# Keys and queries of half batches 4 and 5: direct loads and TensorE transposes in place of casts and transposing loads

## The chip, the cores and the metric

The kernel runs on one core of a Trainium2 chip. A core has a matrix engine (TensorE, PE in the profile; PEld is its weight load), a vector engine (DVE), a scalar engine (ACT), GpSimd (POOL) and a sync engine (SP) that mostly issues DMA transfers. Each engine works through its own list of instructions in order; semaphores order the lists among each other. The metric is the device time of one execution in microseconds. The median of three runs of the kernel before is 398.96 us.

## The reference

Attention with a window of 32 positions to each side, and with 8 global positions that see everything and are seen by everything; then an MLP with the activation h cos(h).

```python
scores = (q @ k.T) / sqrt(D)                 # B, H, S, D = 8, 8, 576, 64
mask = (abs(i - j) <= 32) | is_global[i] | is_global[j]
attn = softmax(where(mask, scores, -1e9))
x = (attn @ v).transpose(0, 2, 1, 3).reshape(B * S, H * D)     # 4608 x 512
h = x @ w_in                                 # w_in 512 x 2048
out = (h * cos(h)) @ w_out                   # w_out 2048 x 512
```

All inputs and the output are float32 in DRAM; the kernel computes in float16 with float32 sums.

## The kernel before

A *pair* is two heads of one batch (32 pairs, `pr`), a *half* is four heads of one batch, so two pairs (16 halves, `s` or `n`). Half n holds pairs 2n and 2n + 1. Halves 4 and 5, which the change is about, hold pairs 8 to 11.

**Attention of one pair.** The queries are cut into 11 blocks of 56. For every block there is a tile of 128 keys (the 8 global ones and 120 around the block) in `kw`, and a tile of queries in `qb`. `scores` multiplies them four blocks at a time into a PSUM tile `st` (L440), ACT takes the exponential `e` (L442), and DVE multiplies it with a mask to `pm` (L443). `values` multiplies `pm` with the values `vw` into `pv` (L452), and DVE normalises to `xn` (L463). `turn_x` transposes `xn` on PE (L475), and DVE copies it into `xT` (L478), the transposed input of the MLP.

**MLP.** `mlp_in`, written "1" in the order, makes one 128 x 512 block of h (L491, four matmuls into `ph`), its cosine on ACT (L494) and the product `g` on DVE (L495). `mlp_out`, written "2", does four matmuls of the second layer into `po` (L505); each fourth one ends with a copy of `po` to `o` (L510 on ACT or L512 on DVE) and a store (L514).

**How kw and qb are filled.** Their 8 global columns come from POOL's copies (L394, L398, L399). The rest is made by `local_k` and `local_q` in one of two ways. For pairs below `2 * HY`, with HY = 4 the pairs 0 to 7, `load_qk` (L260, issued by POOL) brings a half's keys and queries into `kn` and `qn` with positions on partitions, 72 partitions of four heads of 8 rows, converted to float16 on the way. `turned` then transposes them on PE, 16 small transposes for k and 16 for q (L407) into a PSUM tile `t`; ACT copies k into `kw` (L414) and one head of q into `qb`, DVE the other head (L427). For the other pairs `cast_half` (L249 for v, L253 for k and q, issued by POOL) converts a half into float16 scratch in DRAM, `turn_half` (L265 and L266, issued by SP) loads k and q of it with a transposing DMA into `kT` and `qT`, and DVE copies from there (L417, L430).

**Values.** `load_v` and `load_vg` (L308 to L316, issued by SP) fill `vw` of a pair, four buffers in turn, from the scratch that the cast of v wrote, and from the gathered global rows.

**Order of the work.** The schedule is written by hand: the order of calls is the order of instructions on each engine. A first part (FRONT, L674) does pairs 0 to 3 and loads the weights. Then the loop at L684, called the steps here, runs s = 2 to 15; step s does the attention of pairs 2s and 2s + 1 between pieces of the MLP, in the order of the string ORDER (THIRD for s = 2). In it `sa0 sa1 sa2` and `sz0 sz1 sz2` are the scores of the two pairs, `pa` and `pz` their values, `xa` and `xz` their `turn_x`, `n` is a sum of squares on ACT (L524), `G` the casts, and `kc qc kd qd` prepare `kw` and `qb` for the two pairs of the next step. A "1" or "2" with nothing ready does nothing.

`G` is `casts(s)`: POOL waits for the `xn` of the step's second pair (L662), then issues the casts of half s + 2 (with s = 4 also of half 7, and the gather of the second half of the global rows). At the end of step s come `turn_half(s + 2)` and then the values of pairs 2s + 4 and 2s + 5, all on SP, whose list is in order: what stands behind a transposing load waits until the cast that it reads has landed.

PSUM tiles with the tag "s", three buffers in turn, hold `st`, the result of `turn_x` and, in the steps, also `t`. `po` has one buffer in the steps and `ph` has two.

Of the kernel before, what the change touches and what calls it, by code (L numbers as in the profile page):

```python
# [24 lines left out]
W = 120  # L25
BP = 6
KL = 32
HY = 4
RW = 8
KPAD = 4  # L30
KP = KPAD + S // RW + 10
# [23 lines left out]
def dview(ap, offset, *dims):  # L55

    return bass.AP(ap.tensor, ap.offset + offset, [list(d) for d in dims])
# [134 lines left out]
def kernel(  # L192
# [51 lines left out]
    def cast_half(s, which):  # L244

        base = s * 4 * S * D
        for x in which:
            if x == "v":
                nc.gpsimd.dma_start(v16[s * 4 * S : (s + 1) * 4 * S].rearrange("(n r) d -> n (r d)", r=16),  # L249
                                    dview(v, base, (16 * D, 4 * S // 16), (1, 16 * D)))  # L250
            else:
                src, dst = {"k": (k, k16), "q": (q, q16)}[x]
                nc.gpsimd.dma_start(dst[s].rearrange("t (h d) -> t h d", h=4),  # L253
                                    dview(src, base, (D, S), (S * D, 4), (1, D)))

    def load_qk(s):

        base = s * 4 * S * D
        for src, dst in ((k, kn[s % 2][KPAD : KPAD + S // RW]), (q, qn[s % 2][0 : S // RW])):
            nc.gpsimd.dma_start(dst.rearrange("x h r d -> x h (r d)"),  # L260
                                dview(src, base, (RW * D, S // RW), (S * D, 4), (1, RW * D)))

    def turn_half(s):

        nc.sync.dma_start(kT[s % 2][:, :, KL : KL + S], k16[s], transpose=True)  # L265
        nc.sync.dma_start(qT[s % 2][:, :, 0:S], q16[s], transpose=True)  # L266
# [19 lines left out]
    def gather(src, dst, half):  # L286
        rows = src.rearrange("b h s d -> (b h s) d")
        for h in range(2):
            nc.gpsimd.indirect_dma_start(
                out=dst[:, half, h], out_offset=None, in_=rows,  # L290
                in_offset=bass.IndirectOffsetOnAxis(ap=gidx_rows[:, 0:1], axis=0),
                element_offset=(half * 32 + h) * S * D)
# [80 lines left out]
    def build_globals(half):  # L373
        for src, dst in ((kg32, kgT), (qg32, qgT)):
            g16 = work.tile([P, P], FP16, tag="g16")
            nc.scalar.copy(g16, src[:, half].rearrange("x h d -> x (h d)"))
            t = ps.tile([P, 16 * G], FP16, tag="s", bufs=3)
            nc.tensor.transpose(t, g16, ident16)
            nc.scalar.copy(dst[:, 16 * half : 16 * half + 16], t.rearrange("x (n g) -> x n g", g=G))
        nc.scalar.copy(vg16[:, half], vg32[:, half])  # L380
# [20 lines left out]
    def turned(src, pr, n):  # L401

        t = ps.tile([P, RW, n], FP16, tag="h" if front[0] else "s", bufs=2 if front[0] else 3)
        h0 = 2 * (pr % 2)
        for r in range(RW):
            for h in range(2):
                nc.tensor.transpose(t[h * D : (h + 1) * D, r], src[:n, h0 + h, r], ident16[:n, :n])  # L407
        return t

    def local_k(pr):  # L410
        to = kw[pr % NK][:, :, G:]
        if pr < 2 * HY:
            t = turned(kn[pr // 2 % 2], pr, KP)
# [5 lines left out]
    def local_q(pr):  # L419
        if pr < 2 * HY:  # L420
            t = turned(qn[pr // 2 % 2], pr, QP)
        for h in range(2):
            hp = slice(h * D, (h + 1) * D)
            to = qb[pr % NK][hp, :, h, G:]
            if pr < 2 * HY:
                copy = nc.scalar.copy if h == 0 or pr < 2 else nc.vector.tensor_copy
                copy(view(to, (2 * C, NB), (RW, QB // RW), (1, RW)),  # L427
                     view(t[hp], (QB // RW, NB), (1, QB // RW), (QP, RW)))
            else:
                nc.vector.tensor_copy(to, view(qT[pr // 2 % 2][hp, pr % 2], (QB, NB), (1, QB)))  # L430
# [89 lines left out]
    def x_squares(s):  # L520

        sq = work.tile([P, 2 * BP * P], FP16, tag="sq", bufs=1)
        xn = xn_of.pop(s)
        nc.scalar.activation(sq, view(xn, (1, 2 * BP * P)), AF.Square,  # L524
                             accum_out=x_sq[:, s : s + 1])
# [47 lines left out]
    def one(n=1):  # L573
        for _ in range(n):

            if ins_q and ins_q[0][0] < ready[0] and ins_q[0][0] < outs_q[0][0] + 2:
                t, f = ins_q.pop(0)
                mlp_in(t, f)
                ready[1] = t * NF + f + 1

    def two(n=1):
        for _ in range(n):
            t, u = outs_q[0] if outs_q else (NTT, 0)

            need = min(t * NF + 4 * (u % 4) + 12, NTT * NF) if tail[0] else min(t * NF + 4 * (u % 4) + 7, (t + 1) * NF)
            if outs_q and need <= ready[1] and (tail[0] or NTT * NF - len(outs_q) < outs_by[0]):
                mlp_out(*outs_q.pop(0))
# [7 lines left out]
    with tc.manual_schedule():  # L595
# [48 lines left out]
        def load_values(pr):  # L644
            load_v(pr)
            load_vg(pr)
# [9 lines left out]
        def globals_kq(pr):  # L656
            globals_k(pr)
            globals_q(pr)

        def casts(s):  # L660

            nc.gpsimd.tensor_copy(gate, xn_of[s][0:1, 1, 0, 0:1])  # L662
            for n in range(4, 2 * B):
                if s == (n - 2 if n < 7 else n - 3):
                    cast_half(n, "vkq")
            if s == 4:
                for src, dst in ((k, kg32), (q, qg32), (v, vg32)):
                    gather(src, dst, 1)
# [15 lines left out]
        for s in range(2, B * NP // 2):  # L684
            if s == 2:
                nc.gpsimd.dma_start(w_out16, moe_w_out.rearrange("(c p) n -> p c n", p=P))
            outs_by[0] = 4 * (s - 2) if s < 5 else 8 * (s - 3)
            for pr in (2 * s + 2, 2 * s + 3):
                if 8 <= pr < B * NP:
                    globals_kq(pr)  # L690
            for step in (THIRD if s == 2 else ORDER).split():
                if step == "1":
                    one()
                elif step == "2":
                    two()
                elif step == "n":
                    x_squares(s - 1)
                elif step == "G":
                    casts(s)
                else:  # L700
                    f, pr = (STEPS | LOCAL)[step[0]], 2 * s + "azcd".index(step[1])
                    if pr < B * NP:
                        f(pr, *[int(x) for x in step[2:]])
            if s % 2 == 1:
                ready[0] = s // 2 + 1 + (s // 2 == B - 1)
            if s < B * NP // 2 - 2:
                turn_half(s + 2)
                load_values(2 * s + 4)
                load_values(2 * s + 5)
            if s == 5:  # L710
                build_globals(1)
# [49 lines left out]
```

## Time and profile before

The profiled execution has a span of 395.4 us from the first to the last instruction.

| | |
|---|---|
| median of the runs (lowest, highest) | 398.96 us (396.92, 400.0) |
| span of the profiled execution | 395.4 us |
| busy PE, DVE, ACT, POOL | 328.3, 260.6, 238.8, 114.8 us |
| matmuls of the MLP, L491 and L505 | 142.8 and 140.4 us, 576 each |
| transposes of k and q on PE, L407 | 5.7 and 5.3 us, 128 each |
| ACT copies from them, L414 and L427 | 8 x 1257 ns, 10 x 666 ns |
| DVE copies from them, L427 | 6 x 803 ns |
| DVE copies from kT and qT, L417 and L430 | 24 x 556 ns, 48 x 460 ns |
| POOL issuing casts of k and q, L253 | 12 x 1765 ns, 12 x 2304 ns |
| POOL issuing direct loads of k and q, L260 | 4 x 821 ns, 4 x 785 ns |
| DMA queue q1 (issued by SP) | 124,509 packets, 27.89 MB |
| DMA queue q0 (issued by POOL) | 63,952 packets, 18.75 MB |

How to read such a profile: a line of the engine groups names the line of the code, the engine, the operation and the tiles as output<-input; a timeline line begins with the start and the duration in us, and ends in brackets with the time that the engine stood idle before it and what it waited for. Steps 2 to 5 run from 55.47, 74.98, 99.68 and 118.22 us; step 6 begins at 140.05, and from step 8 on a step takes 16.9 us. The loop ends at about 310 us; the rest is MLP.

### The profile page before, as it was taken

The page shows a single profiled execution, that of the slowest core. Times are in us where ns is not written, and L with a number is a line of the kernel's source. Part 1 is how long each engine was busy: PE and PEld are TensorE (multiplying, and loading weights), DVE is VectorE, ACT ScalarE, POOL GpSimd, SP SyncE. Part 2 cuts the span into 40 slices and gives each one's busy share as a digit, 9 for nine tenths or more (in the row PEclk, how much of TensorE's full clock was granted, in tenths as well). Part 3 has the DMA queues.
Part 4 walks back from the last instruction along what each step waited for, and adds up shares of the span by engine and source line. Part 5 has one row for each costly group of instructions (what it writes and reads, how often), then busy time and mean ns, then how long its engine had stood idle before and what let it go on. Part 6 is the DMA issues. An engine that isn't in the chain of part 4 may idle for free.

```text
span 395.4 us, 7373 instructions
## 1 busy us (share of the span) xinstructions
PE 328.3 (83%) x2678; PEld 174.7 (44%) x2678; DVE 260.6 (66%) x600; ACT 238.8 (60%) x351; POOL 114.8 (29%) x250
## 2 busy tenths in 40 slices
PE   0272179576778889899999999999999979999993
PEld 0262164343434355455555555555555334444441
DVE  7744157555687768789788888888889354544300
ACT  1572066945575686677778678776777866244210
POOL 6573032504268275071443507223000100000000
PEclk9997558969999999999999999999999999999999
DMA  6989979999999999999999999999990000010121
GB/s 92 96 123 199 123 43 181 215 130 124 176 121 177 108 175 131 166 154 180 149 176 187 127 177 140 191 141 120 144 118 31 27 2 27 28 54 27 55 80 60
DMA packets 188504, 47.18 MB, mean 119 GB/s; under 512 B 177005, under 2 KB 183405, under 8 KB 188205
## 3 DMA queue, kind: packets, MB, share of 16 engines
q1 hardware_dynamic: 124509, 27.89, 59.6%
q0 software_dynamic: 63952, 18.75, 48.4%
q8 instruction: 23, 0.38, 0.5%
q14 instruction: 20, 0.16, 0.2%
HBM read 47.73 MB, written 21.23 MB: 174 GB/s over the span
## 4 chain that ended last, share of the span: by engine, by line
PE 67%; DMA 10%; DVE 8%; ACT 5%; issue 3%; SPq 3%; another core or an unknown queue 1%; POOL 0%; ACTq 0%; DVEq 0%
PE po L505 28%; PE ph L491 27%; DMA q<-in_q_dram 4%; PE st L440 4%; PE pv L452 4%; DMA vw<-vg 3%; DMA vw<-v 3%; DVE g L495 2%; PE tx L475 2%; SPq L308 2%; ACT cos L494 2%; DVE xn L463 1%; PE t L407 1%; ACT sq L524 1%
## 5 line engine op out<-in xcount | busy, mean ns | idle before, releaser
L491 PE MATMUL ph<-xT,w_in 128*128 128x512 f16 x576 | 142.8, 385 | 6.7 <-DVE g L495 5.9
L505 PE MATMUL po<-w_out,g 128*128 128x512 f16 x576 | 140.4, 380 | 5.0 <-DMA w_out<-in_moe_w_out_dram 3.6
L494 ACT ACTIVATE cos<-ph,pio 128x512 f16<-128x512 f32 x144 | 97.3, 686 | 77.2 <-PE ph L491 75.6
L495 DVE TENSOR_TENSOR g<-cos,ph 128x512 f16<-128x512 f16 x144 | 96.4, 685 | 55.0 <-ACT cos L494 52.7
L505 PEld LDWEIGHTS <-g 128*128 128x128 f16 x576 | 55.4, 98 | 67.7 <-issue 5.2
L491 PEld LDWEIGHTS <-w_in 128*128 128x128 f16 x576 | 54.1, 99 | 69.4 <-issue 13.1
L442 ACT ACTIVATE e<-st 128x512 f16<-128x512 f32 (+1 forms) x96 | 47.6, 561 | 14.3 <-PE st L440 9.3
L443 DVE TENSOR_TENSOR pm<-e,mask 128x512 f16<-128x512 f16 (+1 forms) x96 | 37.0, 405 | 23.8 <-ACT e L442 21.9
L662 POOL COPY gate<-xn 1x1 f16<-1x1 f16 x14 | 2.5, 182 | 143.3 <-DVE xn L463 143.3
L452 PE MATMUL pv<-vw,pm 128*64 128x65 f16 x704 | 20.6, 204 | 23.1 <-issue 10.3
L440 PE MATMUL st<-qb,kw 128*128 128x128 f16 x352 | 30.8, 238 | 4.2 <-ACT e L442 1.5
L440 PEld LDWEIGHTS <-kw 128*128 128x128 f16 x352 | 26.3, 108 | 14.2 <-POOL xT L483 2.9
L463 DVE TENSOR_TENSOR xn<-pv,r_all 128x768 f16<-128x768 f32 x32 | 30.6, 958 | 1.9
L452 PEld LDWEIGHTS <-pm 128*64 128x64 f16 x704 | 16.6, 117 | 27.3 <-issue 19.0
L253 POOL DMA_DIRECT2D q<-in_q_dram x12 | 27.6, 2304 | 0.0
L414 ACT COPY kw<-t 128x1320 f16<-128x1320 f16 x8 | 10.1, 1257 | 28.7 <-PE t L407 28.7
L483 POOL COPY xT<-xg 128x4 f16 x64 | 20.5, 320 | 22.0 <-DVE xT L478 18.6
L510 ACT COPY o<-po 128x512 f32<-128x512 f32 x18 | 10.5, 586 | 22.4 <-PE po L505 21.9
L524 ACT ACTIVATE sq<-xn 128x1536 f16<-128x1536 f16 x16 | 23.6, 1474 | 0.0
L430 DVE COPY qb<-qT 64x616 f16<-64x616 f16 x48 | 22.1, 460 | 0.3
L253 POOL DMA_DIRECT2D k<-in_k_dram x12 | 21.2, 1765 | 0.3 <-issue 0.3
L512 DVE COPY o<-po 128x512 f32<-128x512 f32 x18 | 12.3, 685 | 12.1 <-PE po L505 12.0
(106 smaller groups left out, 269.2 us busy)
## 6 DMA issues: line engine op xcount, KB each, us to landing
out_dram<-o SPq DMA_DIRECT2D x36, 256.0 KB
vw<-v SPq DMA_DIRECT2D x47, 165.0 KB
v<-in_v_dram POOLq DMA_DIRECT2D x16, 288.0 KB
k<-in_k_dram POOLq DMA_DIRECT2D x12, 288.0 KB
q<-in_q_dram POOLq DMA_DIRECT2D x12, 288.0 KB
vw<-v SPq DMA_DIRECT2D x16, 135.0 KB
w_in<-in_moe_w_in_dram POOLq DMA_DIRECT2D x4, 512.0 KB
w_out<-in_moe_w_out_dram POOLq DMA_DIRECT2D x1, 2048.0 KB
```

Source lines behind the costliest of these rows:

```text
L253: nc.gpsimd.dma_start(dst[s].rearrange("t (h d) -> t h d", h=4), dview(src, base, (D, S), (S * D, 4), (1, D)))
L430: nc.vector.tensor_copy(to, view(qT[pr // 2 % 2][hp, pr % 2], (QB, NB), (1, QB)))
L440: nc.tensor.matmul(st[:, j], kp[:, g0 + j], view(qp[:, g0 + j], (1, P)), start=True, stop=True)
L442: nc.scalar.activation(e[:, :n], st[:, :n], AF.Exp, scale=scale)
L443: nc.vector.tensor_tensor(view(pm[:, g0], (1, n * P)), view(e, (1, n * P)), view(mask[:, g0], (1, n * P)), ALU.mult)
L452: nc.tensor.matmul(pv[r0 : r0 + C, j // 6, c0 : c0 + 65], pm[:, j, h], vp[:, j, h], start=True, stop=True)
L463: nc.vector.tensor_tensor(view(xn, (384, 2), (D, 6), (1, D)), view(pv, (512, 2), (65, 6), (1, D)), view(rp, (6, 2), (1, 6), (0, D)), ALU.mult)
L491: nc.tensor.matmul(ph, w_in16[:, j, f * P : (f + 1) * P], xT[:, j, t * TT : (t + 1) * TT], start=(j == 0), stop=(j == NC - 1))
L494: nc.scalar.activation(cos, ph, AF.Sin, bias=pio2)
L495: nc.vector.tensor_tensor(g16[:, f], cos, ph, ALU.mult)
L505: nc.tensor.matmul(po, g16[:, f, s * P : (s + 1) * P], w_out16[:, f], start=(f == 0), stop=(f == NF - 1))
L524: nc.scalar.activation(sq, view(xn, (1, 2 * BP * P)), AF.Square, accum_out=x_sq[:, s : s + 1])
```

## The change

HY goes from 4 to 6. Halves 4 and 5 (pairs 8 to 11) are then prepared as halves 0 to 3 are: `casts(2)` and `casts(3)` issue `load_qk` for them, and of the casts only the one of v, which now comes after those loads. Their `turn_half` is left out. `local_k` and `local_q`, which are not edited, take the transposes on PE for pairs below 12, at the ends of steps 3 and 4. `max(7, HY)` is 7 as before. `kn` and `qn` have two buffers each, which halves 2 and 3 used last in FRONT and in step 2.

```diff
-HY = 4
+HY = 6
@@ casts(s)
             for n in range(4, 2 * B):
-                if s == (n - 2 if n < 7 else n - 3):
-                    cast_half(n, "vkq")
+                if s == (n - 2 if n < max(7, HY) else n - 3):
+                    if n < HY:
+                        load_qk(n)
+                    cast_half(n, "v" if n < HY else "vkq")
@@ end of a step
             if s < B * NP // 2 - 2:
-                turn_half(s + 2)
+                if s + 2 >= HY:
+                    turn_half(s + 2)
                 load_values(2 * s + 4)
                 load_values(2 * s + 5)
```

## The prediction

> **What bounds the kernel now.** I read four things in this order: the slices of the page, the waits, the stretches of the loop's steps, and inside them the timeline of the engines and the packets by queue. Step s means one pass of the loop at line 684; a step ends with the copies that prepare the next step's two head pairs.
>
> The slices of the page (40 slices of 9.9 us) show TensorE:
>
> ```profile
> PE   0272179576778889899999999999999979999993
> PEclk9997558969999999999999999999999999999999
> ```
>
> From slice 15 (about 140 us) PE is full; before that it is not. The next view, each step's stretch with the busy time of PE, PE's weight loads, DVE, ACT and POOL, then granted clock and DMA, says how much:
>
> ```profile
> 74.98:99.68 24.70, 15.19 (x119) 7.91 (x118) 13.05 (x30) 14.22 (x21) 5.30 (x10) 0.86 1.55 145
> 99.68:118.22 18.54, 14.45 (x126) 7.33 (x127) 13.63 (x32) 11.67 (x19) 7.64 (x16) 1.00 1.41 145
> 118.22:140.05 21.83, 17.90 (x145) 9.13 (x146) 16.77 (x38) 13.80 (x22) 12.72 (x18) 1.00 1.69 145
> ```
>
> These are steps 3, 4 and 5. PE is idle for 9.5, 4.1 and 3.9 us in them, and in the later steps (16.9 us each) hardly at all. The change works in steps 2 to 4 only, so a us gained or lost there is carried to the end, one for one, by a PE that is full from then on. What PE waits for, in its timeline:
>
> ```profile
> 79.32 1.49 PE L505 MATMUL po<-w_out,g 128*128 128x512 f16 x4 [3.57 <-DMA w_out<-in_moe_w_out_dram]
> ...
> 83.50 1.02 PE L452 MATMUL pv<-vw,pm 128*64 128x65 f16 x22 [1.52 <-DMA vw<-vg]
> ...
> 91.61 0.76 PE L452 MATMUL pv<-vw,pm 128*64 128x65 f16 x22 [3.03 <-DMA vw<-v]
> ...
> 99.68 0.49 PE L440 MATMUL st<-qb,kw 128*128 128x128 f16 x6 [0.95 <-POOL xT L483]
> ```
>
> The first wait is for the MLP's second weight, issued before anything that the change touches: it stays. The next two, 4.55 us, are for values of pairs 6 and 7, which SP's queue (q1) carries in 128-byte packets while POOL's queue (q0) carries first that weight and then the casts of half 4. For the wait at 91.61 the view names a load of pair 8, which that matmul does not read; the landing records show the globals of pair 7's values, issued at 84.89, landing at 91.7, with the transposing loads of half 4 (issued 85.69 and 88.23) running through the same queue. The wait at 99.68 ends when DVE has copied pair 8 out of qT.
>
> **The change, part by part.** Keys and queries of halves 4 and 5 (pairs 8 to 11): out go 4 casts (2,304 packets each), 4 transposing loads and DVE's copies (4 x 556 ns for kw, 8 x 460 ns for qb, 5.9 us); in come 4 direct loads, 128 transposes on PE, on ACT 4 copies of 1257 ns and 4 of 666 ns, on DVE 4 of 803 ns. In each of steps 3 and 4 that is 3.85 us more ACT work and, by step 2's rows (kn 0.50 and qn 0.45 us for 16), 1.9 us more PE work.
>
> *POOL and SP.* POOL issues the direct loads in 0.82 and 0.79 us against 1.77 and 2.30, ahead of the value cast instead of behind it. Values of half 4 then land some 5 us later than now (at about 85.5), but pair 8 needs them at 105.95: hidden. SP no longer stops at 85.69 to 89.86 and 103.19 to 106.93 for casts, so the loads queued behind them (pairs 8 to 11) start earlier; none of those is waited for now, so this is worth nothing there.
>
> *Term A, the waits for pairs 6 and 7.* The packets by queue in the 6 us beside the weight (72 to 78), and in the 6 us beside half 4's casts (80 to 86):
>
> ```profile
> q0 software_dynamic: 1086, 1.31, 124.8%
> q1 hardware_dynamic: 1013, 0.13, 27.7%
> ...
> q0 software_dynamic: 3998, 0.51, 130.0%
> q1 hardware_dynamic: 2712, 0.34, 72.5%
> ```
>
> Beside 1 KB packets the values move at 1013/6 = 169 packets a us, beside 128-byte casts at 452. The direct loads are 1 KB packets, so they hold q1 back more while they last, and last less. Their duration: half 3's pair, the same transfers, was issued at 38.53 and 39.27 and its landings run from 41.0 to 46.8, 5.8 us; at the weight's rate (1086/6 = 181 a us) 576 packets would take 3.2 us. I take 5.8, the same transfer. q1 moved 2,006 packets from 78.4 to the landing of pair 6 at 83.6. At 169 a us it moves 980 by 84.2 and about 190 beside the 1.1 us value cast; the other 840, at the 1,343 a us that q1 reaches alone (2,687 packets in 92 to 94), take 0.6: pair 6 lands at about 85.8, 2.3 us later than now. From there PE needs the 5.1 us that lie now between 83.50 and 88.58, so it comes to pair 7 at 90.9, when pair 7's packets have drained with no transposing load among them. That is 0.7 us before 91.61: A = -0.7. Bounds: -2.9 if pair 6 lands as now and pair 7's wait goes; +1.5 if the clock stays at half (a rival below).
>
> The Trainium skill ("DMA: Bandwidth & Descriptors", section "Queues, rings and completion order") says that a DMA engine takes turns between queues by packets, so that bytes are not shared fairly; the 169 against 452 agrees, and by that rule alone, without the landings of half 3, the relief would be no larger than A.
>
> *Term B, the end of step 3.* Step 2 already runs such copies, and its ACT rows are my yardstick:
>
> ```profile
> 69.34 1.25 ACT L414 COPY kw<-t 128x1320 f16<-128x1320 f16 x1
> 70.48 0.67 ACT L427 COPY qb<-t 64x616 f16<-64x616 f16 x1
> 71.04 1.27 ACT L494 ACTIVATE cos<-ph,pio 128x512 f16<-128x512 f32 x2
> 72.22 1.25 ACT L414 COPY kw<-t 128x1320 f16<-128x1320 f16 x1
> 73.36 0.67 ACT L427 COPY qb<-t 64x616 f16<-64x616 f16 x1
> ```
>
> A kw copy starts 0.70 us after its first transpose (68.64), the qb copy 1.14 later, the next ACT work 0.56 after that; DVE's qb copy starts only when ACT's has ended (the waits name it 6 times of 6). The transposes use the three "s" buffers of PSUM that the scores use too, so the third score tile of the next step waits for DVE's last qb copy. On today's clock: transposes at 97.42, ACT's copies at 98.12, 99.26, 99.82 and 100.96 to 101.63, DVE's qb to 102.45, then DVE's output copy (0.69), behind it in the queue, to about 103.1. The next step's first group into po, at 101.80 today, waits for that copy: B = +1.4. PE's own 1.9 us fit into the 0.95 and 1.34 us that it idles there now. Bounds 0 and +2.5.
>
> *Term C, the end of step 4.* Two cosines stand between the copies here. Transposes at 114.78, ACT's kw at 115.57, qb 116.71, cosine 117.27, kw 117.87, qb 119.01 to 119.68, cosine, table load, first exponential at 121.5 (today 119.50). DVE's last qb copy ends at 120.5; the third score tile and the po group behind it go at 120.8, today 118.83: C = +2.0. Bounds: +0.5 (PE's 1.9 less the 0.63 and 0.76 it idles) and +3.9 (all of ACT's work).
>
> *Term D.* PE waits 1.19 us at 166.56 for values of pair 15. SP is behind from 121 to 163 by a stream that starts with half 6's cast, issued in step 4 before C; C comes after it, so the stream gains 2 us on PE and the wait goes: D = -1.2. Bounds -1.2 and 0.
>
> Sum: -0.7 + 1.4 + 2.0 - 1.2 = +1.5 us on a span of 395.4 us, so 396.9. The span lies 3.6 us below the median of the runs, 398.96, which I put down to start and end around it; the time is 400.5 us.
>
> **The rivals.**
>
> *Relief wins.* Half 4's transfers are all that holds pairs 6 and 7 back: both waits go (-4.55), D too, and the transposes fit into PE's idle time (B 0, C +0.5): -5.2, 393.7 us. For it: DMA's share is 1.55 in step 3, higher than in step 4. Against it: pair 6's loads were already late behind the weight, before any cast ran. Chance 0.12.
>
> *ACT becomes the bound of steps 3 and 4.* It decides if the exponentials of the next step start more than 2 us later after their scores than now (1.28 us at 118.22; in step 2, with the copies, 3.37). Then ACT's 3.85 us lie on the path twice: 7.7 - 0.7 - 1.2 = +5.8, 404.8 us. For it: in step 2 ACT has no gap over 0.3 us from 68.75 to 79.8. Against it: PE has 2.6 us of po groups to run meanwhile. Chance 0.25.
>
> *The clock stays down.* The granted clock is half from 79.73 to 86.56, after the 3.57 us idle. Its changes lie multiples of 3.41 us apart (31.95 to 35.36 is the shortest piece, 79.73 to 86.56 is two), and the second of the two pieces, from 83.1, was full of work. If pair 6 lands at 85.8, that piece is nearly empty; half clock for 3.41 us more costs 1.7, for 6.82 us 3.4: 402.2 or 403.9 us. The Trainium skill ("TensorE: Matmul & The Clock Gate", Part 1) has a free-running window of 3.4 us that sets the clock, by which this would happen; the trace agrees with its length (6.83 is two of them). Chance 0.16, half for each.
>
> *Hidden anyway.* The waits for pairs 6 and 7 follow the weight alone and stay (A 0): 401.2, inside the forecast's own range. That the change would not do what it says is excluded by the order of instructions of the two kernels: four transposing loads fewer on SP, 128 transposes more on PE.
>
> **How the numbers follow.** My case has 0.47. With bounds taken together it spans about 396.5 to 402.9; the range goes to 405.0 for ACT and the clock and leaves out the relief. One per cent is 4 us, about what three runs that spread from 396.92 to 400.0 can tell. Faster: the relief, 0.12. Slower: ACT and the longer clock case, 0.25 + 0.08 = 0.33. Within: 0.47 + 0.08 = 0.55.
>
> **What would show it.** A: pair 6's first matmul later than 83.5 with pair 7's wait gone. B and C: the po group after the third score tile starts 1.4 and 2 us later after the xz transposes than now, held by a qb copy. D: no wait at pair 15. I am wrong if pair 6 comes no later than now (relief), if the first exponentials of steps 4 and 5 lag by 3.9 us (ACT), or if the clock is 0.5 past 87 us.

## The result, and the profile after

Over 17 runs of each kernel the changed one takes 400.76 us in the median (398.64 to 404.27), the one before 398.28 us (394.74 to 402.08): 1.0089 times as long, 95% interval 1.0062 to 1.0115. That is slower by 0.9%, inside the 1% that the prediction called no change, and 2.5 us between the medians where the forecast had 1.5 between the spans.

The profiled execution of the changed kernel has a span of 398.9 us, 3.5 more than the one before. Its slices of TensorE and of the granted clock:

```profile
PE   0272079569897789999999999999999969999994
PEclk9986558969999899999999999999999999999998
```

Slices are 10.0 us now, counted from 0. PE is full from slice 15 on as before. New are slices 12 and 13 (120 to 140 us): a 7 for PE in each where the row before had 8, and in slice 13 an 8 for the granted clock where it had 9. The prediction has nothing there. Steps 3, 4 and 5 as stretches (columns as before: PE, weight loads, DVE, ACT, POOL, then clock, DMA share, GB/s):

```profile
74.76:100.38 25.62, 16.86 (x184) 9.14 (x182) 12.41 (x27) 15.73 (x23) 5.15 (x18) 0.87 1.15 140
100.38:119.29 18.91, 16.09 (x190) 8.55 (x191) 12.36 (x28) 14.98 (x23) 5.83 (x7) 1.00 0.96 105
119.29:143.32 24.03, 19.26 (x142) 9.42 (x142) 14.88 (x33) 14.26 (x21) 15.19 (x26) 0.93 1.68 136
```

In steps 3 and 4 ACT is busy 1.5 and 3.3 us longer and PE 1.7 us each, the transposes; DMA's share falls from 1.55 to 1.15 and from 1.41 to 0.96. Step 5, which the change does not touch, has grown most: 24.0 us for 21.8, PE idle 4.8.

PE's timeline, at the places of the fence of before and at the two that B and C name:

```profile
79.37 1.86 PE L505 MATMUL po<-w_out,g 128*128 128x512 f16 x4 [3.83 <-DMA w_out<-in_moe_w_out_dram]
...
86.29 1.07 PE L452 MATMUL pv<-vw,pm 128*64 128x65 f16 x22 [3.88 <-DMA vw<-vg]
...
91.32 0.57 PE L452 MATMUL pv<-vw,pm 128*64 128x65 f16 x22
...
102.01 0.33 PE L440 MATMUL st<-qb,kw 128*128 128x128 f16 x3 [1.02 <-DVE qb L427]
102.74 2.75 PE L505 MATMUL po<-w_out,g 128*128 128x512 f16 x12 [0.40 <-DVE o L512]
...
121.49 0.33 PE L440 MATMUL st<-qb,kw 128*128 128x128 f16 x3 [1.02 <-DVE qb L427]
121.66 2.75 PE L505 MATMUL po<-w_out,g 128*128 128x512 f16 x12
...
132.39 0.51 PE L475 MATMUL tx<-ident,xn 128*128 128x128 f16 x6 [3.31 <-DVE xn L463]
```

Pair 6 starts at 86.29 instead of 83.50, and pair 7 at 91.32 without a wait instead of 91.61 with 3.03 us of one. The third score tile of steps 4 and 5 (102.01 and 121.49) waits for DVE's qb copy, and the po group behind it goes at 102.74 (101.80 before) and 121.66 (118.83). In the last line, in step 5, PE waits 3.31 us for DVE's `xn` of the first pair; at the same place it waited 1.45 us before.

Since one PE carries everything, the difference can be cut into stretches between fixed matmuls. "xz" is the first of the six `turn_x` transposes of the step's second pair, "po" the first matmul of the first po group of a step that runs twelve or more in a row (of step 3: the first that waits for the weight):

| us | before | after | difference |
|---|---|---|---|
| start to po of step 3 | 79.32 | 79.37 | 0.0 |
| po to xz of step 3 (term A) | 14.72 | 14.27 | -0.45 |
| xz of step 3 to po of step 4 (B) | 7.76 | 9.09 | +1.33 |
| xz of step 4 to po of step 5 (C) | 6.37 | 8.25 | +1.88 |
| po of step 5 to po of step 6 | 21.86 | 24.14 | +2.28 |
| po of step 6 to po of step 8 (D) | 35.29 | 33.84 | -1.45 |

A to D sum to +1.3 us (forecast +1.5); the other 2.3 are step 5.

### The profile page after: what moved, and what is told of

Read it like the earlier page. It is cut to its first block, busy times and chain, and to the rows that moved or that the text cites. A ratio compares the mean times of both kernels' runs of the same rounds, so it can differ in the third digit from the quotient of the medians.

```text
span 398.9 us, 7625 instructions
## 1 busy us (share of the span) xinstructions
PE 331.6 (83%) x2806; PEld 176.4 (44%) x2806; DVE 258.1 (65%) x592; ACT 245.4 (62%) x359; POOL 110.0 (28%) x250
## 4 chain that ended last, share of the span: by engine, by line
PE 70%; DVE 7%; ACT 6%; DMA 6%; issue 4%; POOL 2%; SPq 2%; another core or an unknown queue 1%; ACTq 0%; POOLq 0%; DVEq 0%
PE po L505 30%; PE ph L491 29%; DMA vw<-vg 6%; PE st L440 4%; PE pv L452 3%; PE tx L475 2%; DVE g L495 2%; ACT cos L494 2%; ACT kw L414 2%; DVE xn L463 1%; SPq L308 1%; DVE qb L427 1%; SPq L316 1%; ACT qb L427 1%
## 5 line engine op out<-in xcount | busy, mean ns | idle before, releaser
L414 ACT COPY kw<-t 128x1320 f16<-128x1320 f16 x12 | 15.1, 1255 | 28.2 <-PE t L407 28.1
L483 POOL COPY xT<-xg 128x4 f16 x64 | 19.1, 298 | 23.1 <-DVE xT L478 19.5
L253 POOL DMA_DIRECT2D q<-in_q_dram x10 | 23.0, 2298 | 0.0
L475 PE MATMUL tx<-ident,xn 128*128 128x128 f16 x192 | 17.3, 231 | 5.2 <-DVE xn L463 5.0
L457 DVE TENSOR_REDUCE dg<-pv 8x2 f32<-8x12 f32 x32 | 4.8, 150 | 22.5 <-PE pv L452 19.1
```

The source lines that it names most:

```text
L414: nc.scalar.copy(view(to, (P, NB), (RW, W // RW), (1, RW)), view(t, (QB // RW, NB), (1, W // RW), (KP, RW)))
L475: nc.tensor.transpose(tx[:, n], xn[:, n], ident16)
```

## The experiments

Three groups of four runs, each group on one chip of its own beside 35 runs of the kernel before, whose medians there were 396.0, 397.43 and 397.49 us. Times, spans and stretches in us; the ratio is to the kernel before on that chip, with its 95% interval.

| run | median | ratio | span | po 3 | A | B | C | step 5 | D |
|---|---|---|---|---|---|---|---|---|---|
| e1_half4 | 397.47 | 1.0030 (0.9995 to 1.0066) | 396.5 | 79.83 | 14.73 | 9.09 | 6.44 | 18.97 | 35.74 |
| e2_half5 | 394.34 | 0.9961 (0.9925 to 0.9998) | 390.7 | 78.61 | 13.32 | 7.73 | 8.26 | 18.97 | 33.84 |
| e3_after_gather2 | 397.59 | 1.0033 (1.0003 to 1.0063) | 395.2 | 80.71 | 14.56 | 9.09 | 8.25 | 18.97 | 33.84 |
| e4_before_gather2 | 394.41 | 0.9950 (0.9915 to 0.9985) | 390.9 | 78.28 | 15.06 | 7.76 | 6.24 | 18.97 | 34.55 |
| e5_swap | 399.51 | 1.0058 (1.0027 to 1.0088) | 396.0 | 78.22 | 14.57 | 7.91 | 7.48 | 24.14 | 33.84 |
| e6_late_k4 | 399.38 | 1.0043 (1.0007 to 1.0080) | 398.3 | 78.27 | 11.72 | 12.48 | 8.25 | 23.70 | 33.84 |
| e7_all | 395.67 | 0.9947 (0.9919 to 0.9974) | 396.5 | 80.57 | 13.57 | 11.31 | 7.49 | 18.96 | 33.84 |
| e8_half5_best | 396.29 | 0.9987 (0.9948 to 1.0026) | 393.3 | 78.69 | 14.17 | 7.73 | 7.48 | 18.96 | 33.84 |
| a2_after | 399.87 | 1.0061 (1.0027 to 1.0095) | 397.4 | 78.96 | 14.94 | 9.09 | 8.25 | 22.04 | 34.40 |
| e1b_half4 | 400.65 | 1.0070 (1.0037 to 1.0103) | 399.6 | 78.81 | 16.46 | 9.18 | 6.43 | 25.43 | 33.84 |
| e2b_half5 | 399.70 | 1.0066 (1.0032 to 1.0100) | 395.2 | 77.12 | 13.34 | 7.73 | 8.25 | 23.23 | 33.84 |
| e9_swap_gather2 | 396.08 | 0.9963 (0.9935 to 0.9992) | 394.0 | 80.19 | 15.96 | 7.90 | 7.48 | 18.97 | 33.84 |

The theory: terms A to D as the prediction has them, plus a stall in step 5 that belongs to the gather of the global rows, which POOL issues there. The rival: the direct loads themselves cause step 5, by what they shift.

**e1_half4 and e2_half5: one half at a time.** HY = 5, so that half 4 alone is loaded directly; and half 5 alone:

```diff
-HY = 6
+HY = 5                         # e1
```

```diff
+DIRECT = (0, 1, 2, 3, 5)       # e2, in place of HY
-        if pr < 2 * HY:
+        if pr // 2 in DIRECT:
...
-                if s + 2 >= HY:
+                if s + 2 not in DIRECT:
```

> Only half 4 goes by the direct loads; half 5 keeps its casts, transposing loads and DVE copies. My theory (terms A to D, each in its own place): pair 6's first matmul late, at about 86.3 us (before 83.5, after 86.3), no wait at pair 7 (91.3 as after), the first po group of step 4 about 1.35 us later after the xz transposes than before (B), and no cost at the end of step 4 (C 0: the po group of step 5 follows the xz transposes of step 4 by 6.4 us as before, not 8.3). Sum near +0.5 us against before, less 1 us if the wait at pair 15 also goes. Rival (the relief needs both halves, or the cost is ACT's work as such): B and C in half each, or pair 6 not late.

> Only half 5 goes by the direct loads; half 4 is cast and loaded transposed as before. My theory: step 3 as before (waits of about 1.5 and 3.0 us for pairs 6 and 7 at 83.5 and 91.6 us, B 0), the end of step 4 costs the 1.9 us of term C (po group of step 5 8.3 us after the xz transposes of step 4, before 6.4), the wait at pair 15 goes (about -1.2). Sum about +0.7 us. Rival (half 5's casts and loads hold back something in step 4 or 5 that the trace of before does not name): faster than before.

B comes with half 4 alone (9.09 for 7.73 to 7.76 without it), C with half 5 alone (8.26 for 6.24 to 6.44). In e2, PE's timeline has C's wait and none of B's (97.57 is the first score group of step 4, all 11 matmuls in one piece):

```profile
97.57 0.77 PE L440 MATMUL st<-qb,kw 128*128 128x128 f16 x11 [0.95 <-POOL qb L399]
...
118.42 0.33 PE L440 MATMUL st<-qb,kw 128*128 128x128 f16 x3 [1.02 <-DVE qb L427]
```

D is half 5's too: the wait at pair 15 stays in e1, and in e2 PE has none there. PE's timeline of e1:

```profile
166.09 0.72 PE L452 MATMUL pv<-vw,pm 128*64 128x65 f16 x22 [1.09 <-DMA vw<-vg]
```

The times did not follow the forecast for e2: it was faster than the kernel before, not a little slower. And in both profiles step 5 took 18.97 us, 2.9 less than in the profile of before, with the gather where it was. So the gather alone does not make the stall.

**e3_after_gather2 and e4_before_gather2: the gather out of step 5**, in the changed kernel and in the one before:

```diff
-            if s == 4:
+            if s == 2:
                 for src, dst in ((k, kg32), (q, qg32), (v, vg32)):
                     gather(src, dst, 1)
```

> The changed kernel with the gather of the second half of the global rows (six indirect DMAs on POOL) issued in step 2 instead of step 4. Theory: the 3.3 us stall of PE in step 5 (132.39 us), which I had not forecast, is there because PE's semaphore updates arrive up to 4.3 us late while POOL issues these indirect DMAs, and only then. Moved, the stall in step 5 falls under 0.5 us, the half clock at 133.7 goes with it (together 4 to 5 us), and late updates appear in step 2 or 3 instead, beside the wait for the second MLP weight, where they cost 0 to 2 us: 2 to 5 us faster than the changed kernel, so 0.5 to 2.5 us faster than before. Rival: the stall is contention with the casts of halves 6 and 7, issued at the same time; then it stays in step 5 and the time stays within 1 us of the changed kernel's.

> The kernel before with the same move of the gather to step 2. Theory (late PE updates while POOL issues indirect DMAs): before has the same stall in step 5, smaller (updates 2.5 us late, PE idle 1.45 us at 127.7); it goes, and the kernel is 0.5 to 3 us faster than before. Rival (contention of the casts): the idle 1.45 us stays and the time is the same.

Step 5 is 18.97 us in both, as in e1 and e2 on this chip with the gather where it was, so these two runs cannot tell the theory from its rival. e3 was expected 0.5 to 2.5 us faster than the kernel before and was slower than it by 0.3%; e4 was faster by 0.5%, as expected, but what made that gain is not shown. Against each other, from their own times, e3 takes 1.0081 times as long as e4, interval 1.0048 to 1.0114. So the change costs about as much where step 5 has no stall in either kernel. The two spans are no pure measure of A to D: of the 4.3 us between them 2.1 are there before the kernels differ (POOL's copy to `gate` in step 2, which stands ahead of the first different instruction, starts at 69.83 us in e3 and at 67.75 in e4), so they belong to the executions and not to the change. B, C, A and D make +1.3, +2.0, -0.5 and -0.7, in all 2.1 us or 0.5%.

**e5_swap: queries before keys.** If B and C are the chain in which DVE's qb copy is the last of four ACT copies and two DVE copies, then turning q first must shorten it, since DVE starts after ACT's short copy:

```diff
+            order = THIRD if s == 2 else ORDER
+            if s in (3, 4):
+                order = order.replace("kc qc", "qc kc").replace("kd qd", "qd kd")
-            for step in (THIRD if s == 2 else ORDER).split():
+            for step in order.split():
```

> The changed kernel with q's transposes and copies ahead of k's at the ends of steps 3 and 4 (qc kc, qd kd). Theory: B and C are the chain ACT kw, qb, kw, qb, then DVE's last qb, at whose end the third score tile gets its PSUM buffer; with q first DVE's copy runs beside ACT's kw copy, and the last link is ACT's kw copy. From the xz transposes of step 3 to the first po group of step 4: 7.8 us (before 7.76, after 9.10); from those of step 4 to the po group of step 5: 7.4 to 7.5 us (before 6.36, after 8.26). In all 2.1 us faster than the changed kernel. Rival (B and C are the amount of ACT and PE work, which stays the same): 9.1 and 8.3 us, same time.

B fell to 7.91, C to 7.48. The chain in the changed kernel, ACT and then DVE:

```profile
97.58 1.26 ACT L414 COPY kw<-t 128x1320 f16<-128x1320 f16 x1 [0.51 <-PE t L407]
98.73 0.67 ACT L427 COPY qb<-t 64x616 f16<-64x616 f16 x1
99.30 1.26 ACT L414 COPY kw<-t 128x1320 f16<-128x1320 f16 x1
100.44 0.68 ACT L427 COPY qb<-t 64x616 f16<-64x616 f16 x1
```

```profile
101.16 0.80 DVE L427 COPY qb<-t 64x616 f16<-64x616 f16 x1 [0.93 <-ACT qb L427]
101.99 0.69 DVE L512 COPY o<-po 128x512 f32<-128x512 f32 x1
```

and DVE in e5:

```profile
99.12 0.80 DVE L427 COPY qb<-t 64x616 f16<-64x616 f16 x1 [0.92 <-ACT qb L427]
99.96 0.69 DVE L512 COPY o<-po 128x512 f32<-128x512 f32 x1
```

In the changed kernel DVE's second qb copy starts 3.58 us after ACT's first copy (97.58), in e5 2.42 after it (96.70); the output copy follows at once in both. The whole time does not show the 2.1 us expected: the ratio is 1.0058 where that of the changed kernel was 1.0089 on another chip, and the two intervals overlap. Step 5 took 24.14 us here, as in the profile after.

**e6_late_k4: half 4's direct loads after pair 6's values.** They leave `casts(2)` and go into step 3 behind `pa`, so that pairs 6 and 7 have q0 free of them:

```diff
-                    if n < HY:
+                    if n < HY and n != 4:
                         load_qk(n)
@@ the loop over the order's pieces
+                    if s == 3 and step == "pa":
+                        nc.gpsimd.tensor_copy(gate, xn_of[s][0:1, 0, 0, 0:1])
+                        load_qk(4)
```

> The changed kernel with the direct loads of half 4 issued in step 3 after pair 6's xn instead of in step 2, so that only the value cast follows the second MLP weight in POOL's queue. Theory for term A: the 1 KB packets of these loads hold pair 6's values back (86.3 us instead of 83.5), and what the casts and transposing loads had held back at pair 7 is lost to that. Moved, pair 6 starts at most 4.2 us after the first po group (after: 6.9) and pair 7 does not wait: xz of step 3 comes 12 to 12.7 us after the first po group (before 14.7, after 14.3), 2 us faster than the changed kernel. Rival (pair 6 is late only through the MLP weight ahead of it): pair 6 still 6.9 us after the first po group, same time. It also gives one more look at step 5, where the gather stays: the stall of PE while POOL issues indirect DMAs appears in some executions and not in others (18.3 us from step 5's first po group to step 6 without it; 21.2 and 23.5 with it).

PE's timeline shows both sides of it:

```profile
82.27 0.76 PE L452 MATMUL pv<-vw,pm 128*64 128x65 f16 x22 [0.97 <-DMA vw<-vg]
...
97.95 0.47 PE L407 MATMUL t<-ident,qn 78*64 78x78 f16 x16 [3.58 <-DMA qn<-in_q_dram]
```

Pair 6 starts 4.0 us after po instead of 6.92, and A's stretch is 2.6 us shorter: the direct loads are what holds the values back. Pair 7, which was expected not to wait, waits 1.30 us. And now the transposes wait 3.58 us for qn, and the clock is 0.50 from 98.79 to 102.20 us behind it. The loads issued late are needed at once, and the wait has only changed its name; the 2 us expected did not come.

**e7_all: e5, e6 and the gather in step 2 together.**

> The changed kernel with q ahead of k in steps 3 and 4, half 4's direct loads after pair 6's xn, and the gather in step 2. If the three repairs add: B 0 (7.8 us), C about 7.45 us, xz of step 3 12 to 12.7 us after the first po group, step 5 18.3 us, no wait at pair 15: against before -2 (A) + 0 + 1.1 (C) - 1.2 (D) less the stall that before has in some executions (0 to 2.9): 2 to 5 us faster than before. Rival (the gather's indirect DMAs in step 2 hold back pair 6 as the direct loads did): xz of step 3 at 14 us and about 1 us faster than before.

**e8_half5_best: half 5 alone, q first in step 4, the gather in step 2.**

> Only half 5 by direct loads, q ahead of k at the end of step 4, the gather in step 2. By the terms: A 0 and B 0 (half 4 is cast as before), C 7.45 us against 6.36 (+1.1), D -1.2, no stall in step 5 (0 to -2.9): 0 to 3 us faster than before. In e2_half5, without the swap and with the gather in step 4, the runs were 0.4% faster than before, where the terms give +0.7 us; if that was the stall missing by chance, this one is faster than before by more than e2's 0.4%.

Both have 18.96 us in step 5, on the chip where e5 and e6 had 24.14 and 23.70. e7 is faster than the kernel before, by 0.5% (about 2 us, the lower end of what was expected). But qn still comes 2.22 us late (B's 11.31), and xz of step 3 comes 13.57 us after po instead of 12 to 12.7, nearer to the rival's 14: pair 6's first matmul starts 4.77 us after po, and the other 21 then wait 1.19 us more for `vw`. e8 did not come out clearly faster: its C is 7.48 as planned, but the twelve matmuls of step 4's po group took 4.2 us instead of 2.75, because they ran at half clock (columns as above):

```profile
96.78:100.19 3.41, 1.44 (x14) 0.78 (x13) 3.32 (x8) 2.15 (x4) 2.39 (x10) 1.00 1.54 184
100.19:103.60 3.41, 3.01 (x8) 1.05 (x8) 1.38 (x4) 0.20 (x1) 0.00 (x0) 0.50 0.90 166
```

e2b below has the same piece of half clock (97.60 to 101.01 us), and e2, the same kernel, has none there.

**a2_after, e1b_half4, e2b_half5 on a third chip**, the changed kernel, e1 and e2 again, to see whether the halves add up and whether step 5 goes with the chip.

> The changed kernel once more, on the same chip as the two halves of the change (next two runs). The ratios so far don't add: half 4 alone +0.3%, half 5 alone -0.4%, both +0.9%, but half 4 and half 5 alone were run together in one job and both in another. In that job no trace has PE's semaphore updates late while POOL issues indirect DMAs, neither at 6 to 14 us, where all kernels issue the same gather, nor in step 5; in the traces of before and after and of e5 to e8 they are late by up to 4 us at both places. Theory: the stall in step 5 belongs to the chip or the execution, not to the change, and without it the change costs B + C + D + A = 1.34 + 1.89 - 1.2 to -1.5 - 0.3, about +1.5 us (+0.4%); with it, as much more as the stall is longer than before's (21.86 and 24.14 us from step 5's first po group to step 6's). In this job the step 5 of these three runs has 24 us if the updates at 10 us are late, and 19.0 if they are not, and the ratio of both halves is the sum of the two to 0.4%.

> Half 4 alone again, beside both halves on one chip: A about -0.1, B +1.34, C 0, D 0: +1.2 us, +0.3%, and step 5 as the run before has it (19.0 or 22 to 24 us).

> Half 5 alone again, beside both halves on one chip: A 0, B 0, C +1.89, D -1.2 to -1.5: about +0.5 us, +0.1%, and step 5 as the two runs before have it. If it is again 0.4% faster than before, the terms miss something that half 5 gains.

B, C and their owners are the same to 0.1 us. The halves do not add up: 0.70% and 0.66% alone, 0.61% together, with step 5 at 25.43, 23.23 and 22.04 us; the sum was expected to hold to 0.4%, and each half alone to cost 0.3% and 0.1%. The kernel before was not profiled on this chip, so how much of this is step 5 stays open. e2's gain on the first chip did not come again with the same kernel here; what made it is not known. What PE waits for in step 5 is DVE, and DVE waits for PE. DVE's timeline of e1_half4, where step 5 is short, and of e1b_half4, the same kernel on the other chip:

```profile
125.49 0.74 DVE L443 TENSOR_TENSOR pm<-e,mask 128x512 f16<-128x512 f16 x2
126.14 0.15 DVE L457 TENSOR_REDUCE dg<-pv 8x2 f32<-8x12 f32 x1
```

```profile
126.27 0.88 DVE L443 TENSOR_TENSOR pm<-e,mask 128x512 f16<-128x512 f16 x2
132.19 0.16 DVE L457 TENSOR_REDUCE dg<-pv 8x2 f32<-8x12 f32 x1 [5.04 <-remote]
```

`dg` reads the `pv` that PE has just filled. In e1 it goes at once; in e1b it goes after 5 us in which DVE stands idle, and the view names nothing of this core's work ("remote"), because PE's matmuls had long ended. The semaphore records of the trace show PE's count of finished work going up 5.9 us after the end of the last `pv` matmul (126.27 to 132.17 us), and `dg` starts right behind. In the profile of the changed kernel it is 4.3 us, and four such updates arrive together between 130.67 and 130.82; ACT's cosine, which waits for them too, starts at 130.79 and `dg` at 130.73. POOL's timeline at that time:

```profile
125.49 1.05 POOL L289 DMA_INDIRECT qg<-in_q_dram,gidx_rows  x1 [0.30 <-issue]
126.85 1.01 POOL L289 DMA_INDIRECT vg<-in_v_dram,gidx_rows  x1 [0.30 <-issue]
128.16 0.95 POOL L289 DMA_INDIRECT vg<-in_v_dram,gidx_rows  x1 [0.30 <-issue]
```

**e9_swap_gather2: the changed kernel with q first and the gather in step 2**, on the chip where a2 has the stall.

> Both halves by direct loads, q ahead of k in steps 3 and 4, and the gather in step 2 (the direct loads of half 4 stay in step 2, unlike in e7_all, where they came 2 to 3 us too late for the transposes). By the terms against before: A -0.3 (14.3 us from the first po group to xz of step 3), B +0.15, C +1.1, D -1.2 to -1.5, no stall in step 5: 0 to -0.5 us without before's stall, up to -3.4 us with it; so 0 to 0.8% faster than before. Rival (the gather in step 2 costs as much in step 3 as it saves in step 5): the same as e5_swap, 0.6% slower than before.

Step 5 is 18.97 us, with no wait on DVE:

```profile
126.93 0.74 DVE L443 TENSOR_TENSOR pm<-e,mask 128x512 f16<-128x512 f16 x2
127.58 0.15 DVE L457 TENSOR_REDUCE dg<-pv 8x2 f32<-8x12 f32 x1
```

From their own times on this chip e9 takes 0.989 times as long as a2 (0.986 to 0.993), and it beats the kernel before by 0.4%, within what was expected. A is 15.96 us, 1.7 more than expected and 1.0 more than in a2; the 3.1 us less in step 5 outweigh that. In all, seven of the nine profiles with the gather in step 5 (before's among them) have late updates there, and both without them are from the first chip; of the five with the gather in step 2 none has them in step 5. On the second and third chip it is five of five with the gather in step 5 and none of three with it in step 2. The casts of halves 6 and 7, the rival of e3, stay in step 4 in all of them, so they do not make the stall by themselves. Late updates also stand beside the first gather, which POOL issues at 6 to 13 us, in all ten profiles that are not from the first chip.

## Why the prediction was right, and where it was not

**A, forecast -0.7, in the two profiles -0.45.** The steps were right: pair 6 at 86.29 (forecast 85.8), then 5.03 us to pair 7 at 91.32 (90.9), and pair 7's wait gone. e6 shows the cause. The size, though, came from one execution. Up to step 3's casts, e2 and e2b run the instructions of before, and e1, e5, a2 and e1b those of after:

| us after po of step 3 | pair 6 | pair 7 | xz |
|---|---|---|---|
| casts of half 4: before, e2, e2b | 4.18, 3.96, 4.54 | 12.29, 10.87, 10.91 | 14.72, 13.32, 13.34 |
| direct: after, e1, e5, a2, e1b | 6.92, 7.18, 7.00, 6.80, 7.54 | 11.95, 12.41, 12.25, 12.62, 14.22 | 14.27, 14.73, 14.57, 14.94, 16.46 |

The means for xz are 13.8 and 15.0: over these executions A is +1.2, inside the prediction's bounds (-2.9 to +1.5) but of the other sign. Most of that is the clock, as the rivals below show. The wait of 3.03 us at pair 7, which A was to save, is the longest of three (1.25 and 2.53 in the others). This was the term whose size failed.

**B and C, forecast +1.4 and +2.0, measured +1.33 and +1.88.** The yardstick of step 2's copies held, in the profiles of e1 and e2 each for itself, and e5 shortened both by undoing the order that makes the chain. That PE's 1.9 us of transposes fit into gaps held as well: nothing more than the chain was lost there.

**D, forecast -1.2, measured -1.45.** The wait at pair 15 went, with half 5 as the cause (it stays in e1). It is a small margin: a2 waits 0.29 us there, and e1b, late from step 5, does not wait. Whether the wait goes because PE comes later, as the prediction has it, or because half 5 moves less through the queues, no run separates.

**The rivals.** Relief did not come: pair 6 was later, not earlier. ACT did not become the bound: it is busy 3.3 us longer in step 4, but PE lost 1.9 there, and the first exponentials of steps 4 and 5 start 1.6 and 1.9 us later after their scores than before, where the rival asked for more than 2. But 1.9 is close. The clock did in part what its rival said, and the sign that the prediction named for being wrong there, a clock of 0.5 past 87 us, is in the profile. Granted clock in pieces of 3.4 us, after (columns: PE, weight loads, DVE, ACT, POOL, clock, DMA share, GB/s):

```profile
79.10:82.50 3.40, 3.04 (x15) 1.65 (x14) 1.01 (x4) 1.31 (x4) 0.00 (x0) 0.50 1.37 225
82.50:85.90 3.40, 0.00 (x0) 0.00 (x0) 0.99 (x3) 1.95 (x3) 0.00 (x0) 1.00 0.75 79
85.90:89.30 3.40, 2.99 (x27) 1.53 (x28) 1.47 (x4) 0.08 (x1) 0.00 (x0) 0.51 0.85 90
```

The second piece was as empty as foreseen, and the third ran at half clock; but the second itself was granted in full, so step 3 has two half pieces now as before. PE was busy for 6.03 us in them (5.29 in those of before, 79.7 to 86.5), and half of the difference, 0.4 us, is what it lost more, where the rival had 1.7. The rule that the prediction weighed from the Trainium skill ("TensorE: Matmul & The Clock Gate", Part 1), a free-running window of 3.4 us, agrees with these edges. In other executions it went as the rival says: e1, e5 and a2 have three half pieces in a row, and e1b has three in all. This is e1:

```profile
80.30:90.54 10.24, 5.67 (x43) 3.07 (x42) 2.89 (x8) 3.42 (x5) 0.00 (x0) 0.50 1.12 120
```

An estimate from such busy times (half of what PE is busy at half clock between po and xz) gives a loss of 2.0 us in the mean of the three profiles with casts in the table above and of 3.2 us in the mean of the five with direct loads; PE's idle time there is 4.2 and 4.5 us. So the waits of pairs 6 and 7 come to about the same in sum, and the clock makes most of the 1.2 us. The prediction had the clock as A's upper bound and as a rival at 0.16, but not in the size of A.

**What the prediction did not have** is step 5, +2.28 us in the profile. The stall was in the profile of before (1.45 us at 127.70, and 2.9 of the stretch), and the prediction read its 3.9 us of idle PE as something that the change does not move. It moved without being touched: 3.31 us of wait, and half clock from 133.7 to 137.1 behind it, which costs 1.7.

**The number.** Two errors nearly cancel. The prediction put 3.6 us around the span; the runs of the changed kernel show 1.7 (400.6 us for a span of 398.9), so the profiled execution of before was some 1.8 us under the median rather than typical, and the forecast on its own basis would be 398.6 us. Against that stood 2.3 us of step 5 and A's spread. That the time came within 0.3 us of the forecast 400.5 is therefore luck; B, C and D are not. The plain sum of the prediction's bounds is 395.4 to 406.9 us; its 396.5 to 402.9 does not follow from them. What of the 0.9% is step 5's share can't be settled: before was profiled only once. e3 against e4, where neither has the stall, came to 0.8% with the gather in step 2, and a2 against the kernel before on its chip came to 0.6%.

## What to carry to other kernels

Where direct loads and transposes replace casts, count the copies out of PSUM as a chain with its last reader, and turn first what the second engine copies. Before a wait's length goes into a sum, see whether it repeats from execution to execution; a term smaller than its spread has no sign. Where step 5 had the stall, the versions with the gather in step 2 did not have it, and none of the versions with direct loads was clearly faster than the kernel without them that has the gather in step 2 (e4, 0.995; the best of them, e7, 0.9947, on another chip).

## What was not expected of the hardware

PE's semaphore updates can arrive up to 5.9 us after the matmul that makes them has ended, several at once, and in these profiles only beside the indirect DMAs that POOL issues. It goes with chip or execution: none over 0.5 us in the four profiles of the first chip, and at worst 3.5 to 5.9 us in each of the other ten, in one of the two gathers. With the second gather in step 2 updates come up to 3.5 us late in e7 and 2.3 in e9, for which ACT stands idle for 1.62 and 0.95 us at worst, and none late in e8; from the `gate` copy of step 2 to the first po these three take 9.8 to 10.9 us, the kernels without it 10.1 to 10.6. Up to two records are missing from a trace at these places, so the pairing of updates with matmuls goes by their order. Why POOL's indirect DMAs do this was not tried.

The clock can drop without an empty piece. In the fourteen profiles, up to 157 us, a piece of 3.41 us at full clock was followed by one at half clock in 31 cases, in which PE was busy for 0 to 0.48 of the piece, and by another at full clock in 307, in which PE was busy for 0.40 or more. Where the edges of the pieces fall on the work differs between executions of the same kernel, as between e2 and e2b.
